# Pooled rows stored once a group, and the even and odd parts of a mixing stored apart and added by the loads

## The chip, the cores and the metric

The kernel runs on one core of a Trainium2 chip. A core has five engines that this text names as the profile does: PE (TensorE, matrix products; PEld are its weight loads), DVE (VectorE), ACT (ScalarE), POOL (GpSimd) and SP (SyncE, which here only issues transfers). Every engine works through its own queue in order, and semaphores hold an instruction until what it needs is there. Transfers run on 16 DMA engines; SP and POOL issue them. Matrix products land in PSUM, which has 8 banks; all else is in SBUF.

The metric is the device time of one execution in microseconds (us). The kernel before takes 1201.57 us (median of 3 runs, 1199.37 to 1205.03).

## The reference

Eight batches of 576 tokens, 8 heads of 64 channels. Each batch goes through attention of two kinds (over means of four neighbouring tokens, repeated four times; and local, within three tokens to either side), the real part of a two-dimensional Fourier transform added to the input, and a normalised feed-forward with 2048 hidden channels.

```python
q_d = q.reshape(B, H, Sd, factor, D).mean(axis=3)      # and k, v; factor = 4
out_d = sm_attn(q_d, k_d, v_d)
out_up = np.repeat(out_d, factor, axis=2)
scores = np.where(np.abs(pos[:, None] - pos[None, :]) < factor, scale * q @ k.T, -1e9)
x = (out_up + softmax(scores) @ v).transpose(0, 2, 1, 3).reshape(B, S, H * D)
X = np.fft.fft(np.fft.fft(x, axis=1), axis=2)
u = x + np.real(X)
un = (u - mean(u)) / np.sqrt(var(u) + 1e-06)
out = u + np.maximum(un @ w_ch1, 0.0) @ w_ch2
```

## The kernel before

**Two stages.** The first computes, batch after batch, the attention and the mixing (the Fourier part) and leaves three addends of u in DRAM: the pooled result `ud`, the local result `ux` and the mixed result `um`, each 577 rows of 512 channels. The second, the feed-forward, takes u in 9 blocks of 512 tokens, four tiles of 128 rows each. It loads a tile of `um` and lets two further transfers add `ux` and `ud` to it on the way in (`Block.load`, L715: part 0 is a plain load from SP, parts 1 and 2 are adding transfers that POOL issues with `accum_op`). Then it normalises and turns the tile (`stats`, `norm`, `turn`, L730 to L762) and runs 16 columns of hidden channels (`first`, `high`, `low`, `second`, L775 to L802). All matrix products of that stage have a high and a low part for precision.

**Pooled attention** (`Pooled`, L243): four steps of two heads; the result is gathered in the SBUF tile `odt` (two halves of 72 groups). `store` (L331) writes every group to four rows of `ud`, so that `ud` has a row for each token; `pack` (L341) moves part of `odt` for the mixing.

**Local attention** (`Unit`, L362): five units per batch, with results in `xa` (front half of the sequence) and `xb` (back half, mirrored).

**Mixing** (`Mix`, L514): sums and differences of the halves (L524, L527), folding of channels (`channels` L535, `fold` L548), a split into high and low (L559, L562), products along the sequence into `y` (L584), and products along the channels into PSUM banks `mix` (L616, L623). For each of three slots of rows there is an even and an odd bank. The token n and its mirror image are even plus odd and even minus odd: `even_out` (L627) copies the even bank to SBUF on ACT, and `unfold` (L631) makes sum and difference on DVE, reading the odd bank twice. Both read or write the two halves of a bank alternately, to bring the channels into their order. `store` (L643) writes them to `um`, front rows and mirrored rows, in ten transfers.

**Weights.** The feed-forward's weights come as 64 quarters of 64-bit words and are decoded on the way (`Quarter`, L138: ACT, POOL, three passes on DVE, ACT, POOL). Places for the first 3 of 16 columns exist from the start and are decoded during the first stage; the others follow when the first stage's memory is free (`close_a`, `close_e`, `close_d`).

**Order.** Every step is entered in a list with a number (`at(t, fn)`), and the list is sorted by it. The numbers come from the table `AT` at the head of the file. They are no times; they only set the order in which instructions stand in the engines' queues. `PACE` (20) is the distance of two batches in these numbers.

## Time and profile before

| | |
|---|---|
| median of 3 runs | 1201.57 us |
| profiled execution, whole | 1200.32 us |
| its span, first to last instruction | 1198.5 us |
| mean granted clock of PE | 0.972 |
| moved by DMA | 130.40 MB |
| 12 matrix products of one hidden column, L782, in the feed-forward | 2.72 us |

The profile gives for each engine its busy time, for each group of instructions the mean duration and what ended the idle time ahead of it, and for a stretch of time the busy time of all engines. A wait "PE tpn L753 <- DVE un L745" says that PE stood still until that DVE instruction was done. Tile names follow the program (`o` is the unfolded result, `ut` a tile of u, `un` the normalised tile, `tpn` its transpose, `hps`, `hh` and `hl` a hidden column with its high and low part). The rows themselves are shown in the prediction.

### The profile page before, as it was taken

Reading aid. Unit: us, or ns where it says so; the run is one execution under the profiler, and the core shown is the slowest. Engines: PE = TensorE matmul, PEld = TensorE weight load, DVE = VectorE, ACT = ScalarE, POOL = GpSimd, SP = SyncE. Lnnn points to the kernel's source line nnn. Section 1 sums busy time; section 2 is a strip of 40 time slices with the busy share of each in tenths; the row PEclk is TensorE's granted clock in tenths of the full one; section 3 lists DMA queues with packets and bytes.
Section 4 is the critical chain, followed back from the end, with each engine's and each line's share of the span. In section 5 each row is a group of like instructions: output and inputs, shape, how many; then the busy total and the mean of one; then the engine's idle time right before and its main releaser. Section 6 shows DMA issues by size and latency. Waiting matters only on the chain.

```text
span 1198.5 us, 20501 instructions
## 1 busy us (share of the span) xinstructions
PE 1128.4 (94%) x8224; PEld 949.5 (79%) x8224; DVE 590.6 (49%) x1234; ACT 363.7 (30%) x1054; POOL 307.7 (26%) x410
## 2 busy tenths in 40 slices
PE   4879988899976999999999999999999999999998
PEld 4768877888875788888888888888888888888887
DVE  3698999999878989632321321321321322222111
ACT  3556675667643444311111111111111111111010
POOL 2155436335547556320300200300200300200000
PEclk7889998999997999999999999999999999999999
DMA  8586777778868454160600600600600600600000
GB/s 270 176 249 200 223 227 232 196 226 277 204 159 200 103 161 125 60 141 1 141 1 1 141 1 1 141 1 1 141 1 1 141 1 1 141 1 1 36 1 36
DMA packets 61631, 130.40 MB, mean 109 GB/s; under 512 B 7560, under 2 KB 7688, under 8 KB 61280
## 3 DMA queue, kind: packets, MB, share of 16 engines
q1 hardware_dynamic: 48016, 99.30, 26.1%
q0 software_dynamic: 13520, 29.79, 14.3%
q8 instruction: 65, 1.06, 0.3%
q14 instruction: 30, 0.25, 0.1%
HBM read 90.13 MB, written 37.80 MB: 107 GB/s over the span
## 4 chain that ended last, share of the span: by engine, by line
PE 74%; DVE 11%; DMA 6%; issue 4%; POOL 2%; ACT 1%; SPq 1%; DVEq 0%; POOLq 0%; ACTq 0%
PE hps L782 32%; PE acc L802 11%; PE acc L800 11%; PE acc L801 11%; PE y L584 3%; DMA vsum<-in_vg_dram 2%; DVE w L535 1%; DVE o L636 1%; PE tpn L753 1%; DMA ux<-xa 1%; DVE xs L524 1%; PE av L462 1%; DVE sums L389 1%; DMA raw<-in_wq_dram 1%; PE sc L403 1%
## 5 line engine op out<-in xcount | busy, mean ns | idle before, releaser
L790 DVE SCALAR_TENSOR_TENSOR hl<-hps,hh 128x512 fp32r<-128x512 f32 x144 | 99.4, 691 | 463.0 <-ACT hh L786 463.0
L782 PE MATMUL hps<-unT,w1h 128*128 128x512 f32 x1152 | 311.6, 392 | 1.7 <-DVE unT L762 1.0
L782 PEld LDWEIGHTS hps<-unT,w1h 128*128 128x128 f32 x1152 | 215.1, 188 | 47.8 <-DVE unT L762 1.3
L786 ACT ACTIVATE hh<-hps 128x512 fp32r<-128x512 f32 x144 | 86.2, 598 | 543.4 <-PE hps L782 543.4
L800 PE MATMUL acc<-w2h,hh 128*128 128x512 f32 x576 | 226.4, 393 | 0.0
L802 PE MATMUL acc<-w2h,hl 128*128 128x512 f32 x576 | 225.1, 391 | 0.0
L801 PE MATMUL acc<-w2l,hh 128*128 128x512 f32 x576 | 225.0, 391 | 0.0
L782 PE MATMUL hps<-unT,w1l 128*128 128x512 f32 x576 | 155.2, 391 | 0.0
L782 PEld LDWEIGHTS hps<-unT,w1l 128*128 128x128 f32 x576 | 108.1, 188 | 23.8
L802 PEld LDWEIGHTS acc<-w2h,hl 128*128 128x128 f32 x576 | 108.2, 188 | 23.6
L800 PEld LDWEIGHTS acc<-w2h,hh 128*128 128x128 f32 x576 | 108.2, 188 | 22.8
L801 PEld LDWEIGHTS acc<-w2l,hh 128*128 128x128 f32 x576 | 108.2, 188 | 22.8
L738 POOL TENSOR_TENSOR rstd<-rstd,mhalf 128x1 f32<-128x1 f32 x36 | 20.4, 568 | 307.9 <-DVE rstd L737 306.9
L725 POOL DMA_DIRECT2D ut<-ux x40 | 35.7, 1106 | 205.7 <-DMA ut<-um 205.5
L421 ACT ACTIVATE sb<-sc,mx 128x64 f32<-128x64 f32 x320 | 70.0, 330 | 1.3
L403 PEld LDWEIGHTS sc<-qkT 64*64 64x64 f32 x1280 | 48.0, 146 | 3.8 <-issue 1.2
L462 PE MATMUL av<-vaug,pT 64*64 64x65 f32 x1280 | 46.7, 224 | 4.1 <-DMA vaug<-in_vw_dram 4.0
L762 DVE TENSOR_TENSOR unT<-tpn,unT 128x512 fp32r<-128x512 f32 x36 | 24.7, 687 | 51.3 <-ACT unT L759 51.3
L562 POOL TENSOR_TENSOR fl<-xeo,fh 128x512 fp32r<-128x512 f32 x32 | 44.8, 1401 | 13.7 <-ACT fh L559 13.7
L403 PE MATMUL sc<-qkT 64*64 64x64 f32 x1280 | 48.0, 230 | 0.0
L389 DVE TENSOR_REDUCE sums<-qkT 128x224 f32<-128x896 f32 (+4 forms) x48 | 43.2, 943 | 8.6 <-DMA qkT<-in_qk_dram 8.6
L462 PEld LDWEIGHTS av<-vaug,pT 64*64 64x64 f32 x1280 | 42.9, 140 | 5.4 <-DMA vaug<-in_vw_dram 4.5
(95 smaller groups left out, 1474.2 us busy)
## 6 DMA issues: line engine op xcount, KB each, us to landing
qkT<-in_qk_dram SPq DMA_DIRECT2D x40, 512.0 KB
raw<-in_wq_dram SPq DMA_DIRECT2D x64, 256.0 KB
vaug<-in_vw_dram SPq DMA_DIRECT2D x40, 260.0 KB
ud<-odt SPq DMA_DIRECT2D x16, 576.0 KB
out_dram<-ut SPq DMA_DIRECT2D x36, 256.0 KB
ut<-um SPq DMA_DIRECT2D x32, 256.0 KB
ut<-ux POOLq DMA_DIRECT2D x32, 256.0 KB, 5.7
ut<-ud POOLq DMA_DIRECT2D x32, 256.0 KB, 5.3
```

Source lines behind the costliest of these rows:

```text
L389: nc.vector.tensor_reduce(out=to, in_=x[:, :, a - g0 : e - g0], axis=AX.X, op=ALU.add)
L403: nc.tensor.matmul(sc[r, a * W : (a + 1) * W], self.qkT[r, 0, a // 2, o : o + W], self.qkT[r, 1, a // 2, o : o + W], start=False, stop=Tru ...
L421: nc.scalar.activation(out=self.sb[:, a], in_=self.sc[:, a * W : (a + 1) * W], func=AF.Exp, scale=0.125, bias=self.mx[:, a : a + 1],)
L462: nc.tensor.matmul(av[r, a, :], pT[r, 4 * hh + a], va[r, 4 * hh + a, :], start=True, stop=True)
L562: nc.gpsimd.tensor_sub(out=self.fl[:, t], in0=self.x[t], in1=self.fh[:, t].bitcast(F32))
L584: nc.tensor.matmul(y, l, r, start=(i == 0), stop=(i == len(mms) - 1))
L782: nc.tensor.matmul(hps, a[:, c, :], unT[:, x, c, :], start=(i == 0), stop=(i == len(mms) - 1))
L786: nc.scalar.activation(out=hh, in_=self.hps[f], func=AF.Relu)
L790: nc.vector.scalar_tensor_tensor(out=hl, in0=self.hps[f], scalar=0.0, in1=self.hh[f].bitcast(F32), op0=ALU.max, op1=ALU.subtract)
L800: nc.tensor.matmul(acc, hh, w2h, start=start, stop=False)
L801: nc.tensor.matmul(acc, hh, w2l, start=False, stop=False)
L802: nc.tensor.matmul(acc, hl, w2h, start=False, stop=stop)
```

## The change

Three things are changed.

1. `Pooled.store` writes each group once, to a `ud` of 144 rows. The load of the feed-forward reads every such row four times (a step of 0 in the access pattern).
2. `even_out` and `unfold` are replaced by `out`, which ACT runs: it copies the even bank once and the odd bank twice, the second time times -1. The even part goes to an array of its own, `ue` (289 rows), and plus and minus odd go to `um`. The middle row of the sequence falls away from one side, so that all arrays but `ue` have 576 rows. The load of a tile has four parts now: `ue` plain, then `um`, `ux` and `ud` adding (`PARTS = 4`).
3. The table `AT` has new numbers throughout.

```diff
-    "mix": (25.73, 25.9, 24.42, 25.37, 25.13),
+    "mix": (25.86, 25.59, 25.55, 25.23, 25.56),
...
-    "add": (17.46, 2.29, 3.72),
+    "add": (10.11, 2.63, 2.76),
...
+PARTS = 4
...
-    ud = [dram.tile([S + 1, DM], F32, name=f"ud{b}") for b in range(B)]
-    ux, um = ([dram.tile([S + 1, DM], F32, name=f"{n}{b}") for b in range(B)] for n in ("ux", "um"))
+    ud = [dram.tile([G, DM], F32, name=f"ud{b}") for b in range(B)]
+    ux, um = ([dram.tile([S, DM], F32, name=f"{n}{b}") for b in range(B)] for n in ("ux", "um"))
+    ue = [dram.tile([S // 2 + 1, DM], F32, name=f"ue{b}") for b in range(B)]
...
-            for t in range(2):
-                r0 = t * (HS + 1)
-                nc.sync.dma_start(
-                    out=ud[self.b][r0 : r0 + HS, :].rearrange("(g r) c -> g r c", r=4),
-                    in_=odt[:GH, t, :DM].unsqueeze(1).to_broadcast([GH, 4, DM]),
-                )
-            nc.sync.dma_start(out=ud[self.b][HS : HS + 1, :], in_=odt[GH - 1 : GH, 1, :DM])
+            nc.sync.dma_start(out=ud[self.b].rearrange("(t g) c -> g t c", t=2), in_=odt[:GH, :, :DM])
...
-        def even_out(self, t):
-            even = self.even[t] = pf.tile([P, DM], F32, name="even", bufs=2)
-            nc.scalar.copy(out=even[: slots[t][1]], in_=self.ps[t, 0])
-
-        def unfold(self, t, minus):
+        def out(self, t, odd, minus):
+
+            i = 1 + minus if odd else 0
             if t == 0:
-                self.o[minus] = pf.tile([P, NSL, DM], F32, name=f"o{minus}", bufs=1)
+                self.o[i] = pf.tile([P, NSL, DM], F32, name=f"o{i}", bufs=1)
             n = slots[t][1]
-            even, ps = (x.rearrange("p (two n) -> p n two", two=2) for x in (self.even[t][:n], self.ps[t, 1]))
-            nc.vector.tensor_tensor(
-                out=self.o[minus][:n, t].rearrange("p (n two) -> p n two", two=2),
-                in0=even,
-                in1=ps,
-                op=ALU.subtract if minus else ALU.add,
+            nc.scalar.mul(
+                out=self.o[i][:n, t].rearrange("p (n two) -> p n two", two=2),
+                in_=self.ps[t, odd].rearrange("p (two n) -> p n two", two=2),
+                mul=-1.0 if minus else 1.0,
             )
...
-            at(u + step + store, self.store, um, self.o)
+            at(u + step + store, lambda: self.store(ue, [self.o[0]]))
+            at(u + step + store, lambda: self.store(um, [self.o[1], self.o[2]]))
...
-                src = (um, ux, ud)[part][b][k0 : k0 + m, :]
+                if part == 0:
+
+                    m = min(m, HS - k0) if k0 < HS else m
+                    j = k0 if k0 < HS else k0 - HS + 1
+                    src = ue[b][j : j + m, :]
+                elif part < 3:
+                    src = (um, ux)[part - 1][b][k0 : k0 + m, :]
+                else:
+                    src = ud[b][k0 // 4 : (k0 + m) // 4, :]
+                    src = bass.AP(tensor=src.tensor, offset=src.offset, ap=[src.ap[0], [0, 4], src.ap[1]])
...
-                    at(starts[n] + 6 + 0.5 * i + 2.5 * part, blocks[n + 1].load, i, part)
+                    at(starts[n] + 6 + 0.5 * i + 1.5 * part, blocks[n + 1].load, i, part)
```

The order that comes out of the list is shown at three places. The first is ACT's queue while the sixth batch is mixed; `sb` and `sd` are the exponentials of the local and the pooled attention, `pT` and `ptd` copies of their transposes, `fh` the high part of a folded slot. Before:

```order
L629 COPY even<-mix 128x512
L572 CAST z<-odt 128x2
L559 CAST fh<-xeo 128x512
L419 ACTIVATE mx<-mx 128x8
L421 ACTIVATE sb<-sc,mx 128x64 x8
L276 ACTIVATE mxd<-mxd 72x4
L281 ACTIVATE sd<-sp,mxd 72x144 x4
L629 COPY even<-mix 128x512
L453 COPY pT<-tpl 128x512
L302 COPY ptd<-tp 72x288 x2
```

With the change (line numbers are those of the changed file; `o_5184` is the even part, the other two are plus and minus odd):

```order
L630 ACTIVATE o_5184<-mix 128x512
L416 ACTIVATE mx<-mx 128x8
L418 ACTIVATE sb<-sc,mx 128x64 x8
L630 ACTIVATE o_5224<-mix 128x512
L630 ACTIVATE o_5228<-mix 128x512
L279 ACTIVATE mxd<-mxd 72x4
L284 ACTIVATE sd<-sp,mxd 72x144 x4
L556 CAST fh<-xeo 128x512
L630 ACTIVATE o_5184<-mix 128x512
L450 COPY pT<-tpl 128x512
L630 ACTIVATE o_5224<-mix 128x512
L305 COPY ptd<-tp 72x288 x2
```

Where one copy of the even bank stood between two groups of exponentials, two copies of the odd bank follow it, the first pair right between `sb` and `sd`.

The second place is DVE's queue at the end of the first stage: the last slots of the last batch are folded (`xs`, `w`, `xeo`), the first block of the feed-forward gets its statistics and its normalised tiles `un`, and the seventh batch is unfolded. Before:

```order
L548 TENSOR_TENSOR xeo<-w 128x256
L524 TENSOR_TENSOR xs<-xa,xb 128x512
L734 BN_STATS st_5975<-ut_106 128x6
L735 BN_AGGR mv<-st_5975 128x2
L737 TENSOR_SCALAR rstd<-mv 128x1
L636 TENSOR_TENSOR o_5831<-even,mix 64x512
L636 TENSOR_TENSOR o_5833<-even,mix 64x512
L745 TENSOR_SCALAR un<-ut_103,mv,rstd 128x512
L535 TENSOR_TENSOR w<-xs 128x255
L535 TENSOR_TENSOR w<-xm 128x255
```

With the change:

```order
L545 TENSOR_TENSOR xeo<-w 128x256
L532 TENSOR_TENSOR w<-xs 128x255
L532 TENSOR_TENSOR w<-xm 128x255
L738 BN_STATS st_5996<-ut_114 128x6
L739 BN_AGGR mv<-st_5996 128x2
L741 TENSOR_SCALAR rstd<-mv 128x1
L545 TENSOR_TENSOR xeo<-w 128x256
L749 TENSOR_SCALAR un<-ut_111,mv,rstd 128x512
L749 TENSOR_SCALAR un<-ut_112,mv,rstd 128x512
```

The unfolding is gone, and the first normalised tile comes after the last folding instead of ahead of it.

The third place is POOL's queue at the handover, where it issues the additions for the second block's tiles (`ut_5951` to `ut_5954` before, `ut_5958` to `ut_5961` now), between the clamps `wt` and the low parts `w1l`, `w2l` of the weight decoding. Before, from the first additions to the second:

```order
L725 DMA ut_5953<-ux_66 128x512
L725 DMA ut_5954<-ux_66 128x512
L164 TENSOR_SCALAR wt<-wt 128x256
L193 TENSOR_TENSOR w1l_5962<-wt,w1h_5961 128x256
L164 TENSOR_SCALAR wt<-wt 128x256
L193 TENSOR_TENSOR w1l_5962<-wt,w1h_5961 128x256
L164 TENSOR_SCALAR wt<-wt 128x256
L725 DMA ut_5951<-ud_57 64x512
L725 DMA ut_5951<-ud_58 64x512
```

With the change, from the second additions to the third:

```order
L729 DMA ut_5960<-ux_66 128x512
L729 DMA ut_5961<-ux_66 128x512
L196 TENSOR_TENSOR w2l_5971<-wt,w2h_5970 128x256
L167 TENSOR_SCALAR wt<-wt 128x256
L196 TENSOR_TENSOR w2l_5971<-wt,w2h_5970 128x256
L167 TENSOR_SCALAR wt<-wt 128x256
L729 DMA ut_5958<-ud_57 64x1x512
L729 DMA ut_5958<-ud_58 64x1x512
```

Ahead of this piece stands a further group of five, for `um`, so that the five of `ud` come two clamps and two low parts later in the queue than before, and after ten other additions instead of five.

More of the change, by code (lines that the diff above doesn't have):

```diff
@@ L22 @@
 AT = {
-    "pooled": (-1.26, -1.46, -2.33, -2.53, -2.33),
-    "mix": (25.73, 25.9, 24.42, 25.37, 25.13),
-    "local_steps": (0, 1.47, 4, 5, 5.98, 8.33, 9.86),
-    "pooled_steps": (0, 1.18, 2.76, 4.04, 5.01, 7.14, 8.75),
-    "qk": (-10, 1.23),
-    "sums": (-2.83, 0.45),
-    "sum_v": (-10.41, -6.5, -3.44, 1.78),
-    "load_v": (4.22,),
-    "store_pooled": (0.83,),
-    "pooled_splits": (0.67, 1.6, 0.62, 0.96, 0.89, 1.28, 3.06),
-    "halves": (0.2, 1.82, -1.06, 1.66),
-    "splits": (0.89, 2.15, 0.3, 0.93, 0.62, 1.76, 2.52),
-    "z": (1.66, 5.51, 6.35, 6.73, 7.91),
-    "sequence": (8.13, 2.44, 0.74, 1.7),
-    "mixed": (16.48, 1.37, 1.17, 1.26, 1.31, 5.81),
-    "store_local": (1.87,),
-    "ffn": (5.97, 1.6),
-    "decode": (37.71, 6.9, 4.1, 1.25, 4.33),
-    "decode_steps": (-1.3, -0.25, 0.38, 2.09, 2.74),
-    "first_norms": (1.77, 1.54, 6.94, 0.87),
-    "second_norms": (0.62, 1.28, 3, 1.2),
-    "add": (17.46, 2.29, 3.72),
+    "pooled": (-1.41, -2.13, -2.53, -2.08, -2.33),
+    "mix": (25.86, 25.59, 25.55, 25.23, 25.56),
+    "local_steps": (0, 1.5, 4, 5.22, 6.36, 8.75, 10.11),
+    "pooled_steps": (0, 1.18, 2.29, 3.46, 4.56, 7.1, 8.75),
+    "qk": (-9.94, 1.51),
+    "sums": (-3.53, 0.27),
+    "sum_v": (-12.81, -9.36, 0.57, 2.2),
+    "load_v": (3.18,),
+    "store_pooled": (1.87,),
+    "pooled_splits": (0.57, 4.65, 0.32, 1.05, 1.04, 3.42, 4.78),
+    "halves": (0.3, 1.87, -1.3, 1.18),
+    "splits": (0.71, 2.15, 0.3, 0.59, 1.81, 2.46, 2.75),
+    "z": (1.06, 5.11, 6.1, 7.81, 9.01),
+    "sequence": (8.04, 2.24, 1.36, 1.52),
+    "mixed": (16.48, 1.35, 1.34, 0.77, 1.23, 5.7),
+    "store_local": (2.79,),
+    "ffn": (5.97, 1.61),
+    "decode": (34.88, 6.9, 3.53, 1.24, 3.62),
+    "decode_steps": (-0.95, -0.64, 0.38, 2.31, 2.97),
+    "first_norms": (4.11, 1.21, 9, 0.37),
+    "second_norms": (2, 1.04, 2.54, 1.7),
+    "add": (10.11, 2.63, 2.76),
 }
@@ L688, in plan @@
                 at(u, self.mix, i, 0)
-                at(u + even, self.even_out, i)
+                at(u + even, self.out, i, 0, 0)
                 at(u + step, self.mix, i, 1)
-                at(u + step + plus, self.unfold, i, 0)
-                at(u + step + minus, self.unfold, i, 1)
-            at(u + step + store, self.store, um, self.o)
+                at(u + step + plus, self.out, i, 1, 0)
+                at(u + step + minus, self.out, i, 1, 1)
+            at(u + step + store, lambda: self.store(ue, [self.o[0]]))
+            at(u + step + store, lambda: self.store(um, [self.o[1], self.o[2]]))
             at(4 * (NPAIR * self.b + NPAIR - 1) + AT["local_steps"][-1] + AT["store_local"][0], self.store, ux, (xa, xb))
@@ L879 @@
     for i in range(TILES):
-        for part in range(3):
+        for part in range(PARTS):
             at(120 + AT["add"][0] * part + 4 * i, blocks[0].load, i, part)
@@ L895 @@
             for i in range(TILES):
-                for part in range(3):
-                    at(starts[n] + 6 + 0.5 * i + 2.5 * part, blocks[n + 1].load, i, part)
+                for part in range(PARTS):
+                    at(starts[n] + 6 + 0.5 * i + 1.5 * part, blocks[n + 1].load, i, part)
                 v = starts[n] + 12 + i * (t - starts[n] - 18) / TILES
@@ L1029, in _tokens @@
     t = np.arange(SEQ)
-    return rows[:, np.where(t <= SEQ // 2, t, SEQ + SEQ // 2 - t)]
+    return rows[:, np.where(t < SEQ // 2, t, SEQ + SEQ // 2 - 1 - t)]
 def kernel(**inputs):
```

5 lines of the change are left out of this document (3 added, 2 removed).

## The prediction

> **What bounds the kernel now.** I read the page's busy row and its 40 slices first, to see where the time is.
>
> ```profile
> span 1198.5 us, 20501 instructions
> PE 1128.4 (94%) x8224; PEld 949.5 (79%) x8224; DVE 590.6 (49%) x1234; ACT 363.7 (30%) x1054; POOL 307.7 (26%) x410
> PE   4879988899976999999999999999999999999998
> DVE  3698999999878989632321321321321322222111
> PEclk7889998999997999999999999999999999999999
> ```
>
> Each slice is 30 us. From slice 14 on PE is full and DVE has time to spare: that is the feed-forward. Ahead of it, DVE reads 9 almost everywhere, and so does PE. In slice 12 (about 360 to 390 us) PE falls to 6 while DVE is still high. The windows give both stretches in numbers: attention and mixing, the handover, its end, and the feed-forward.
>
> ```profile
> core 0: us, PE busy (x) PEld busy (x) DVE busy (x) ACT busy (x) POOL busy (x), PEclk, DMA share, GB/s
> 0.00:353.00 353.00, 304.88 (x4528) 271.85 (x4529) 293.52 (x686) 214.80 (x757) 147.67 (x189) 0.93 0.77 220
> 353.00:369.00 16.00, 0.83 (x6) 0.61 (x5) 15.76 (x26) 1.82 (x4) 11.57 (x12) 0.63 0.86 248
> 369.00:417.00 48.00, 45.04 (x235) 37.78 (x234) 41.57 (x85) 21.20 (x51) 29.78 (x45) 0.95 0.56 132
> 417.00:1198.00 781.00, 777.62 (x3461) 639.26 (x3459) 239.79 (x441) 125.89 (x242) 118.64 (x166) 1.00 0.23 54
> ```
>
> In the last 781 us PE idles 3.4 us. Nothing that spares DVE can shorten that, so the change lives in the first 417 us. There I cut windows from one batch's zero-column product (L600, one per batch) to the next, which gives one period per batch:
>
> ```profile
> 73.55:117.64 44.09, 39.83 (x581) 35.31 (x581) 39.50 (x91) 29.48 (x107) 18.77 (x24) 0.96 0.72 214
> 117.64:158.80 41.16, 36.09 (x535) 32.13 (x532) 38.47 (x93) 26.43 (x91) 19.40 (x23) 1.00 0.80 238
> 158.80:202.92 44.12, 39.56 (x581) 35.02 (x582) 40.27 (x95) 28.45 (x100) 19.45 (x25) 0.93 0.76 217
> 202.92:246.25 43.33, 39.51 (x568) 35.01 (x566) 40.57 (x92) 26.80 (x94) 19.88 (x24) 0.91 0.75 214
> 246.25:285.43 39.18, 36.71 (x576) 33.27 (x575) 35.32 (x83) 26.82 (x96) 17.88 (x21) 1.00 0.80 228
> 285.43:325.89 40.46, 37.38 (x573) 33.51 (x574) 36.01 (x86) 26.32 (x94) 19.98 (x23) 1.00 0.87 243
> ```
>
> The first four periods also decode weights on DVE. They have 38.5 to 40.6 us of DVE in 41.2 to 44.1 us, 90 to 94%, and PE is nearly as full. The last two have 35 to 36 us of DVE and last 39 to 40.5 us. So the period follows DVE's load until PE's own work, 36.7 to 37.4 us at a full clock, stands in the way. ACT has 26 to 29 us and is free for a third of the time. The chain of waits, cut to 240 to 345 us, agrees: it runs through both engines in turn.
>
> ```profile
> by line: PE y L584 10.7%; DVE w L535 8.6%; DVE o L636 7.6%; issue 6.0%; DVE xs L524 5.2%; DMA ud<-odt 5.0%; DVE sums L389 4.9%; DMA odt<-odt 4.7%; DVE mxd L270 4.2%; PE av L462 3.7%; DVE xeo L548 3.3%; PE sp L265 3.0%; PE avd L310 3.0%; DVE
> ```
>
> The unfolding (DVE o L636) has 7.6% of these 105 us, 8.0 us in some 2.6 periods: about 3 us a period stand on the chain.
>
> Then comes the handover. In its 16 us DVE is busy for 15.76 and PE waits for one instruction of it:
>
> ```profile
> 368.52 0.87 PE L753 MATMUL tpn<-ident,un 128*128 128x128 f32 x3 [15.17 <-DVE un L745]
> 356.91 1.29 DVE L636 TENSOR_TENSOR o<-even,mix 128x512 f32<-128x512 f32 x2
> 365.55 1.29 DVE L636 TENSOR_TENSOR o<-even,mix 64x512 f32<-64x512 f32 x2
> 366.76 1.61 DVE L745 TENSOR_SCALAR un<-ut,mv,rstd 128x512 f32<-128x512 f32 x1
> ```
>
> **What the change costs and saves, part by part.**
>
> *The unfolding leaves DVE.* These are the passes that go, the pass that ACT makes now, and a DVE pass over PSUM in plain order:
>
> ```profile
> L636 DVE TENSOR_TENSOR o<-even,mix x48: 673/687/712, 99.3 to 416.3; 128x512 f32<-128x512 f32 x32, 64x512 f32<-64x512 f32 x16
> L629 ACT COPY even<-mix x24: 569/588/637, 97.8 to 409.1; 128x512 f32<-128x512 f32 x16, 64x512 f32<-64x512 f32 x8
> L806 DVE TENSOR_TENSOR ut<-acc,ut 128x512 f32<-128x512 f32 x44 | 27.6, 682 | 2.1 <-PE acc L802 2.1
> ```
>
> Six passes a batch at 0.687 us are 4.1 us less of DVE in each period. ACT gets nine passes a batch where it had three: six more at 0.588 us, 3.5 us, which takes it from 27.4 us (mean of the six rows) to about 31 of 40. The new passes read PSUM alternately from two halves. No ACT row shows that, so I bound it: 0.588 us (L629, plain order) below and twice that above. I take 0.588, because DVE's alternating pass (0.687) costs what its plain one does (0.682). The Trainium skill (SBUF — State Buffer, "Door 1: The DMA port swizzle") speaks against this: PSUM has 8-byte lines, and accesses that leave a line pay for it. By that the pass would come near the upper bound, which is the third rival below; the two DVE rows do not bear it out.
>
> The four decoding periods drop from a mean of 39.7 us of DVE to 35.6, which is the load of the two clean ones (35.3 and 36.0). I let them last what those last, 39.8 on average: 172.7 - 4 x 39.8 = **13.5 us** saved. The clean two drop to 31.5 us of DVE, and PE at 37.0 stays. Some of their 2.8 us above PE is latency that no lighter DVE removes, so I take half: 2 x 1.4 = **2.8 us**. The sum of both, 16.3 us in six periods, is 2.7 us a period, close to the 3 us that the chain gives. The bounds of these two terms together are 4 us, if PE's order is the limit already, and 172.7 + 79.6 - 6 x 37.0 = 30 us, if every period falls to PE's work.
>
> *The end of the front.* Up to 353 us the seventh period is a clean one, about 1 us. Then the chain on DVE loses the seventh batch's three pairs, which stand among the statistics and the last halves: 3 x 1.24 = 3.7 us. All of DVE's work there is queued in a row, so PE's 15.17 us shrink to about 11.5. What is late next is the last folding and the first normalisation, again on DVE. Together **4.7 us**, bounds 2 and 8.
>
> *Stores.* The pooled result is written once instead of four times, the mixing gets five more small stores per batch.
>
> ```profile
> 346.18 1.70 SPq L335 DMA_DIRECT2D ud<-odt  x2
> 347.93 1.56 SPq L339 DMA_DIRECT2D ud<-odt  x1
> 355.33 2.26 SPq L654 DMA_DIRECT2D ux<-xb  x4
> 357.64 0.43 SPq L655 DMA_DIRECT2D ux<-xb  x1
> ud<-odt SPq DMA_DIRECT2D x16, 576.0 KB
> 63.12 7.39 DMA ux<-xa
> ```
>
> SP loses about 2.4 us of issuing per batch (two of three pooled stores) and gains 2.7 (four stores and the row ahead). In bytes, 1.15 MB of pooled rows become 0.29, and the mixing grows by 0.59: slightly less traffic. In the chain of waits a store of the local result (7.39 us) stands behind the pooled one in the second batch; it may land sooner. I take **0**, with 3 us of gain and 2 of loss as bounds.
>
> *A fourth link in the loads.* Each tile of the feed-forward's input is now loaded once and added to three times, not twice. These rows show what one link costs:
>
> ```profile
> L725 POOL DMA_DIRECT2D ut<-ux x40: 806/1006/2127, 297.1 to 1027.7; - x40
> DMA to landing us min/median/max: 3.2/5.3/9.9
> DVE st L734 <- DMA ut<-ud: 4.7, 5, 1.5
> DVE hl L790 <- ACT hh L786: 463.0, 126, 4.9
> ```
>
> That is 1 us of POOL's time per addition and 5.3 us until it lands. In the feed-forward the first statistics of a block already wait for the last addition (5 waits, 4.7 us in all), so they come about 5 us later. Behind them on DVE stands hl for the next column. DVE idles up to 4.9 us ahead of nearly every hl, and PE runs another column in between, so I take **0** there. If that cover failed, the price would be up to 5 us in each of seven blocks.
>
> The second block's loads at the handover are the tighter place:
>
> ```profile
> 374.95 4.42 POOL L725 DMA_DIRECT2D ut<-ux  x5
> 384.93 2.62 POOL L725 DMA_DIRECT2D ut<-ud  x3
> 392.26 0.69 DVE L734 BATCH_NORM_STATS2 st<-ut 128x6 f32<-128x512 f32 x1
> 399.74 0.61 PE L753 MATMUL tpn<-ident,un 128*128 128x128 f32 x4
> ```
>
> POOL issues the first additions at 375, the second at 385; the statistics come at 392 and PE turns the result at 400. A third group between them puts five more issues (4.4 us), and with the clamps and low parts between groups 5 to 10 us, ahead of the statistics. The gap from 392 to 400 covers most of it. Behind the waiting statistics DVE queues weight decoding and hl, for which PE waits. Against it, the last batch's six passes leave DVE here too, 4 us, but PE idles only 3 us of the 48. I take a net **loss of 3 us**, bounds a gain of 3 and a loss of 10. By the Trainium skill (DMA: Bandwidth & Descriptors, "Anatomy of one DMA — SWDGE (gpsimd) path": 2 us fixed plus the bytes) an addition of 256 KB would land after some 2.6 us, an estimate from that page, and the loss would be nearer 1 us; the trace's 5.3 us decides.
>
> *The order of the stages.* PE's order in a period and the start up to 73 us keep their sequence but for swaps of neighbours; **0**, within the bounds above.
>
> **Sum:** -13.5 - 2.8 - 4.7 + 0 + 3 = -18.0 us. The profiled execution took 1200.3 us (span 1198.5 and 1.8 around it), so it becomes 1182.3. The median of the runs is 1.25 us above it: **1183.6 us**.
>
> **Rivals.**
>
> *PE is the limit already.* PE has 36 to 40 us in every period and its order is fixed. Then only the handover gains, 4.7, and about 4 of the periods, less 3: 1196 us. For it: PE is over 90% busy. Against it: the decoding periods are longer just where DVE has more, and in three of the four the clock of 0.91 to 0.96 says that PE pauses.
>
> *Everything falls to PE's work.* 30 us from the periods, 4.7 from the end, loads hidden: 1167 us. Against it: latency remains in any order.
>
> *ACT becomes the bound (slower).* If an alternating pass costs over 1.3 us, ACT gets 9 x 1.3 - 3 x 0.59 = 10 us more per batch, 37 to 39 in all, and the exponentials queue behind the passes. From that point a period exceeds today's, because PE waits for ACT's exponentials and for the banks. At 1.5 us a pass ACT has 39.1 us; with the 4 us that a period now adds to DVE's load, that is 43.1 against today's mean of 42.1, 8 us longer in eight batches, and the loads' 3 us on top: 1201.6 + 11 = 1212 us. For it: nine passes stand among the exponentials of three units. Against it: the DVE rows above.
>
> *The sums are not what is hidden.* The passes go to ACT, but the loads at the handover cost their full 10 us and the periods give only half: 1201.6 - 8 - 4.7 + 10 = 1199 us, no change.
>
> **How the numbers follow.** My forecast (1174 to 1193) gets 0.58, PE as the limit 0.12, PE's work alone 0.15, ACT as the bound 0.06, the loads 0.09. The range leaves out the slower rival and the tail of the best: 1168 to 1201. A measurement tells about 0.5% from no change, 6 us. Faster by more: the forecast, the best case, and a third of PE as the limit, and a little of the loads, 0.78. Within it: 0.15. Slower by more: 0.07.
>
> **What the new profile would show.** No DVE group at 0.69 us from mix; 72 ACT passes near 0.59 us (over 1.0 would mean the third rival). Windows from yz to yz near 39.8 us in the decoding batches and 38.4 after, with PE over 36 in each. PE's one long wait before tpn near 11 us instead of 15.2. In the handover, waits of DVE's statistics for the loads of ud, and a few us of PE behind them. Feed-forward stretch unchanged at 781 us from the second block on. I would be wrong if the periods stay at 41 to 44 while DVE's busy time falls, or if the waits of PE name ACT.

## The result and the profile after

The changed kernel takes **1243.59 us** (median of 4 runs, 1242.69 to 1244.84); the kernel before, run beside it, 1201.44. The ratio is 1.036, 95% interval 1.034 to 1.038: 42 us slower, where 18 us less were predicted. The two profiled spans differ by as much, 1241.5 against 1198.5 us.

Here is the page of the changed kernel: the busy row, and PE in 40 slices of 31 us.

```profile
PE 1145.1 (92%) x8224; PEld 954.6 (77%) x8224; DVE 559.4 (45%) x1186; ACT 385.7 (31%) x1102; POOL 346.4 (28%) x450
...
PE   4988999897878999999899999899899899999998
```

DVE lost what it should: 590.6 us became 559.4, ACT gained 22. But PE's row, which read 9 from slice 14 to the last but one, now falls to 8 four times in that stretch.

The windows of both kernels at the same four marks say where the 43 us of the profiles are: the first product of the feed-forward (hps), and the ends of its first three rounds' results (finish). First the changed kernel, then the one before.

```profile
0.00:377.88 377.88, 316.88 (x4566) 276.58 (x4566) 287.15 (x680) 239.81 (x812) 171.79 (x213) 0.94 0.76 213
377.88:457.88 80.00, 74.80 (x355) 60.74 (x355) 63.60 (x129) 36.10 (x87) 49.36 (x75) 1.00 0.64 159
457.88:514.66 56.78, 56.05 (x248) 46.35 (x248) 43.24 (x82) 22.41 (x54) 29.14 (x44) 1.00 0.31 89
514.66:1241.50 726.84, 697.41 (x3059) 570.96 (x3057) 165.37 (x299) 87.38 (x150) 96.05 (x121) 0.98 0.26 54
```

```profile
0.00:376.69 376.69, 312.73 (x4566) 278.11 (x4566) 315.72 (x721) 220.92 (x771) 163.88 (x207) 0.91 0.76 219
376.69:451.01 74.32, 72.03 (x347) 59.80 (x348) 64.73 (x132) 31.52 (x78) 45.32 (x69) 1.00 0.55 143
451.01:508.73 57.72, 57.72 (x256) 47.81 (x255) 44.52 (x85) 23.40 (x56) 29.50 (x45) 1.00 0.32 92
508.73:1198.50 689.77, 685.89 (x3059) 563.78 (x3057) 165.68 (x299) 87.87 (x150) 68.97 (x90) 1.00 0.21 46
```

The columns are those of the prediction's windows. The front is 1.2 us longer, though DVE has 28.6 us less in it; the handover is 5.7 us longer; and the last row, with the same 3059 products, is **37.1 us** longer. PE idles 29.4 us there instead of 3.9, and its products themselves take 11.5 us more at a mean clock of 0.98.

The groups of waits in the feed-forward (from 420 us on; total, times, longest) name the reason:

```profile
DVE st L738 <- DMA ut<-ud: 37.8, 7, 6.5
PE tpn L757 <- DVE un L749: 25.5, 7, 4.7
```

Seven waits of DVE's statistics for the last addition, seven of PE for what comes of them. One of the seven in order of time, POOL, SP, DVE and then PE of the changed kernel (start, length, engine, line, operation, and the wait ahead of it):

```profile
772.92 3.23 SPq L731 DMA_DIRECT2D ut<-ue  x6
778.42 3.46 POOL L729 DMA_DIRECT2D ut<-um  x4 [34.44 <-DMA ut<-ue]
782.70 0.89 POOL L729 DMA_DIRECT2D ut<-ux  x1 [0.82 <-DMA ut<-um]
787.68 0.95 POOL L729 DMA_DIRECT2D ut<-ud  x1
...
786.08 0.69 DVE L794 SCALAR_TENSOR_TENSOR hl<-hps,hh 128x512 fp32r<-128x512 f32 x1 [4.88 <-ACT hh L790]
793.24 0.69 DVE L738 BATCH_NORM_STATS2 st<-ut 128x6 f32<-128x512 f32 x1 [6.46 <-DMA ut<-ud]
795.08 0.55 DVE L749 TENSOR_SCALAR un<-ut,mv,rstd 128x512 f32<-128x512 f32 x1 [0.74 <-POOL rstd L742]
...
795.68 1.11 PE L757 MATMUL tpn<-ident,un 128*128 128x128 f32 x4 [4.69 <-DVE un L749]
```

The four links start at 772.9, 778.4, 782.7 and 787.7, some 5 us apart, and the statistics start 20.3 us after the first. They stand in DVE's order where three links (15 us) would have been enough: DVE waits 6.46 us. PE's next work, 4 transposes of that very tile, stands close behind in PE's order and cannot start: 4.69 us. It is not hl that PE waits for.

### The profile page after: what moved, and what is told of

It is laid out like the page before. It is cut to its first block, busy times and chain, and to the rows that moved or that the text cites. A ratio compares the mean times of both kernels' runs of the same rounds, so it can differ in the third digit from the quotient of the medians.

```text
span 1241.5 us, 20635 instructions
## 1 busy us (share of the span) xinstructions
PE 1145.1 (92%) x8224; PEld 954.6 (77%) x8224; DVE 559.4 (45%) x1186; ACT 385.7 (31%) x1102; POOL 346.4 (28%) x450
## 3 DMA queue, kind: packets, MB, share of 16 engines
q0 software_dynamic: 18768, 39.23, 18.3%
## 4 chain that ended last, share of the span: by engine, by line
PE 59%; DMA 15%; DVE 13%; POOL 5%; issue 4%; SPq 2%; ACT 2%; POOLq 0%; DVEq 0%; ACTq 0%
PE hps L786 23%; PE acc L804 8%; PE acc L805 8%; PE acc L806 8%; DMA ut<-ud 4%; DMA vsum<-in_vg_dram 3%; POOL ut L729 3%; DMA ut<-ue 2%; PE av L459 2%; PE y L581 2%; DMA ut<-ux 2%; PE sc L400 2%; DMA odt<-odt 1%; SPq L648 1%; PE tpn L757 1%
## 5 line engine op out<-in xcount | busy, mean ns | idle before, releaser
L804 PE MATMUL acc<-w2h,hh 128*128 128x512 f32 x576 | 230.9, 401 | 0.7 <-DVE ut L810 0.7
L806 PE MATMUL acc<-w2h,hl 128*128 128x512 f32 x576 | 228.1, 396 | 1.0 <-DVE hl L794 1.0
L805 PE MATMUL acc<-w2l,hh 128*128 128x512 f32 x576 | 228.6, 397 | 0.0
L729 POOL DMA_DIRECT2D ut<-um x40 | 37.8, 1101 | 210.0 <-DMA ut<-ue 209.2
L763 ACT CAST unT<-tpn 128x512 fp32r<-128x512 f32 x36 | 20.9, 584 | 127.9 <-PE tpn L757 127.9
L459 PEld LDWEIGHTS av<-vaug,pT 64*64 64x64 f32 x1280 | 42.2, 139 | 13.3 <-issue 11.6
L757 PE MATMUL tpn<-ident,un 128*128 128x128 f32 x144 | 24.6, 301 | 28.3 <-DVE un L749 26.9
L559 POOL TENSOR_TENSOR fl<-xeo,fh 128x512 fp32r<-128x512 f32 x32 | 47.3, 1478 | 5.3 <-ACT fh L556 5.3
```

What stands on the lines that cost most here:

```text
L459: nc.tensor.matmul(av[r, a, :], pT[r, 4 * hh + a], va[r, 4 * hh + a, :], start=True, stop=True)
L559: nc.gpsimd.tensor_sub(out=self.fl[:, t], in0=self.x[t], in1=self.fh[:, t].bitcast(F32))
L729: nc.gpsimd.dma_start(out=u[r0 : r0 + m], in_=src, accum_op=ALU.add)
L757: nc.tensor.transpose(tp[:, c * P : (c + 1) * P], self.un[i][:, c * P : (c + 1) * P], ident)
L804: nc.tensor.matmul(acc, hh, w2h, start=start, stop=False)
L805: nc.tensor.matmul(acc, hh, w2l, start=False, stop=False)
```

## The experiments

Each ratio is to the kernel before, run beside it on the same chip. Differences between two kernels are those of their ratios times 1200 us.

### The feed-forward: one link, one place

**e1_late_stats**, the changed kernel:

```diff
-                v = starts[n] + 12 + i * (t - starts[n] - 18) / TILES
+                v = starts[n] + 16 + i * (t - starts[n] - 22) / TILES
```

> The changed kernel with one edit: each block's statistics, normalisation and turn of the next block's first tile stand 4 units (6.8 us by 5.44 us per column of 3.2 units) later in the feed-forward. Theory A (the fourth link lands after the place of the statistics; DVE waits 4.2 to 6.5 us for ud, PE then 3 to 4.7 us at tpn): DVE's waits for ud fall from 41.8 to under 5 us, PE's waits for un vanish, blocks are 89.6 us apart again, and the time falls by the 37 us that seven blocks had grown: 1207 us (1203 to 1213). Rival B (the added loads slow PE's clock or the queues whatever the place): blocks stay at 93 to 96 us and the time within 8 us of 1244. Rival C (the wait only moves to the new place, because POOL issues the links late): half of the loss stays, near 1225.

Measured 1202.83 us, ratio 1.0006 (0.9977 to 1.0035): 42.7 us less than the changed kernel. That is more than the 37 us by which the feed-forward had grown; the two profiles differ in the front too (372.2 us to the first hps against 377.9), which the edit does not touch. One block, from finish to finish (its neighbours are alike):

```profile
659.20:748.83 89.63, 89.63 (x402) 73.73 (x401) 21.88 (x42) 11.71 (x20) 12.61 (x16) 1.00 0.28 59
```

PE is full again in 89.6 us; in the changed kernel such blocks take 92.9 to 96.0. All four links are still there, with the same bytes. Theory A holds; the queues and the clock (B) and a wait that moves along (C) do not.

**e2_before_link**, the kernel before with the fourth link alone:

```diff
-                for part in range(3):
-                    at(starts[n] + 6 + 0.5 * i + 2.5 * part, blocks[n + 1].load, i, part)
+                for part in range(4):
+                    at(starts[n] + 6 + 0.5 * i + 1.5 * part, blocks[n + 1].load, i, part)
...
-                src = (um, ux, ud)[part][b][k0 : k0 + m, :]
+                src = (um, ux, ud, ud)[part][b][k0 : k0 + m, :]
```

> The kernel before with one edit: from the third block on, each tile of the feed-forward's input gets a fourth load (the pooled rows are added a second time, so the input is not the reference's there), spaced 1.5 units as in the changed kernel. Nothing else of the change is in it. Theory A (the fourth link alone makes the loss): seven blocks grow from 89.6 to 93 to 96 us, time 1201 + 30 to 40 = 1231 to 1241. Rival (the loss needs the new order, the ACT passes or the smaller pooled rows): within 6 us of 1201.

Measured 1237.97 us, ratio 1.029 (1.027 to 1.031), 35 us more. Its waits from 420 us on:

```profile
DVE st L734 <- DMA ut<-ud: 38.1, 7, 5.7
PE tpn L753 <- DVE un L745: 25.8, 7, 4.0
```

These are the two groups of the changed kernel, in the kernel before, from one more load a tile. Nothing else of the change is needed for the loss.

**e3_before_early_stats**, the other way round, the place without the link:

```diff
-                v = starts[n] + 12 + i * (t - starts[n] - 18) / TILES
+                v = starts[n] + 9 + i * (t - starts[n] - 18) / TILES
```

> The kernel before with one edit: the same statistics and what follows them stand 3 units (5.1 us) earlier in each block of the feed-forward; three links as before. Theory A (only the distance between the landing of the last link and the place of the statistics counts): DVE waits some 5.5 us for ud and blocks grow by 3 to 6 us, time 1222 to 1240, though nothing of the change is in it. Rival (the number of links or DVE's idle time counts, not the place): within 6 us of 1201.

Measured 1201.61 us, 1.0002 (0.9979 to 1.0026). This says nothing against theory A, since the edit did more than it was meant to: at 9 units the first tile's statistics stand ahead of its last load (11 units) in the program, so they had only two links to wait for. **e9_early_stats_mended** puts all loads ahead:

```diff
-                    at(starts[n] + 6 + 0.5 * i + 2.5 * part, blocks[n + 1].load, i, part)
-                v = starts[n] + 12 + i * (t - starts[n] - 18) / TILES
+                    at(starts[n] + 6 + 0.5 * i + 1.5 * part, blocks[n + 1].load, i, part)
+                v = starts[n] + 9.1 + i * (t - starts[n] - 18) / TILES
```

> The kernel before once more with early statistics. In e3_before_early_stats the first tile's statistics stood ahead of its last load in the program, so they did not wait for it (and left out the pooled rows). Here the three loads of a tile are spaced 1.5 units as in the change, which puts all of them ahead of the statistics, and these stand 2.9 units (4.9 us) earlier. Theory A (only the distance between the last landing and the place of the statistics counts): DVE waits 4 to 6 us a block for ud, PE 2.5 to 4.5 at tpn, 1201 + 20 to 37 = 1221 to 1238. Rival (three links leave room enough, since the closer spacing lets them land earlier): within 6 us of 1201.

Measured 1235.11 us, 1.032 (1.026 to 1.038). DVE waits 35.1 us for ud from 420 us on, and PE 21.4 us at tpn. Three links and statistics 4.9 us earlier lose about what four links lose in the old place. What counts is the distance from the first load to the statistics, in links.

### The front: the order

**e4_old_order**: the code of the change, the table of the order from before (loads at the front 11.64 and 2.48 apart, so that four take the place of three).

```diff
-    "pooled": (-1.41, -2.13, -2.53, -2.08, -2.33),
+    "pooled": (-1.26, -1.46, -2.33, -2.53, -2.33),
...
-    "add": (10.11, 2.63, 2.76),
+    "add": (11.64, 2.29, 2.48),
```

> The changed kernel with the table of the order from before (the spacing of the early loads shrunk so that four take the place of three: 11.64 and 2.48). Theory A (the order is worth nothing in the feed-forward and costs some 10 us at the end of the front, through the local values that wait 8.6 us behind 15 mixing stores): blocks stay at 93 to 96 us, the end of the front gains: 1230 to 1240. Rival (the new table was needed for the new passes, and the old one delays PE by ACT's passes at other places): slower than 1244, 1250 to 1270.

Measured 1261.01 us, 1.047 (1.042 to 1.052): 13 us slower than the changed kernel. The rival was right: with the new passes and stores the old order is worse, and the new one earned these 13 us. A cut of the chain of waits of this run, from the first of a batch's fifteen mixing stores on SP to the last, and what follows:

```profile
168.06 0.41 SPq L648
...
179.16 6.57 DMA vaug<-in_vw_dram
185.86 2.00 PE av L459 x32
```

The local values stand on SP behind 11 us of stores, and PE behind the values. The changed kernel has that too, in its sixth period (SP's issues, then PE):

```profile
287.40 6.51 SPq L648 DMA_DIRECT2D ue<-o  x4
...
303.89 1.08 SPq L649 DMA_DIRECT2D um<-o  x1
305.02 3.42 SPq L372 DMA_DIRECT2D vaug<-in_vw_dram  x2
...
312.81 2.00 PE L459 MATMUL av<-vaug,pT 64*64 64x65 f32 x32 [8.57 <-DMA vaug<-in_vw_dram]
```

The fifteen stores hold SP from 287.4 to 305.0 us, and PE waits 8.57 us.

**e5_even_on_act** (on e1) and **e6_old_order_even_on_act** (on e4) take the five new stores off SP:

```diff
-            at(u + step + store, lambda: self.store(ue, [self.o[0]]))
+            at(u + step + store, lambda: self.store(ue, [self.o[0]], nc.scalar))
...
```

> The changed kernel with the later statistics of e1_late_stats, and the five stores of the even parts (ue) issued by ACT instead of SP, so that SP issues as many mixing stores a batch as before the change. Theory D (SP's issues stand in order, and the five added stores delay the local values and heads behind them): the periods shorten by up to 1 us each and PE's waits for vaug go; 1194 to 1200 against 1203. Rival P (PE's own work and small waits on DVE and POOL set the period in the new order; SP has room): within 3 us of 1203, or slower by the issues that ACT now makes (some 3 us a batch of an engine that has 30 of 41 us).

> The kernel of e4_old_order (the changed code in the order of before, 1261 us, first hps of PE at 395.3 us where before has 376.7) with the five stores of the even parts issued by ACT. Theory D (in the old order a burst of 15 mixing stores, 10.6 us of SP at 168 us, stands ahead of the local values and the heads, and is on the chain of waits with 20% of two periods): the first hps comes 12 to 18 us earlier and the time is 1243 to 1249. Rival (the ACT passes themselves are in the wrong place in the old order): the first hps stays within 5 us, time 1256 to 1266.

Measured 1215.86 us, 1.012 (1.008 to 1.015), and 1287.74 us, 1.072 (1.068 to 1.076): 13 and 30 us slower than their bases; e6 is slower than either forecast. Theory D was not tested by this, because ACT paid. A cut of ACT in e5:

```profile
171.80 3.47 ACTq L648 DMA_DIRECT2D ue<-o  x3
175.31 0.58 ACTq L649 DMA_DIRECT2D ue<-o  x1
175.93 0.42 ACT L587 CAST yh<-y 128x320 fp32r<-128x320 f32 x1 [5.55 <-DMA ue<-o]
```

ACT stands 5.55 us here until its own store lets it go on, and 42.2 us in seven such waits of 3.7 to 12.2 us in all. But it showed something else: ACT, busy for 31 of 41 us, does not hide such waits. So I asked for the price of each engine's time by itself.

### The front: what each engine's time is worth

**e7_dve_passes** and **e10_act_passes** (on e1) put six idle passes a batch on one engine:

```diff
+            if odd:
+                nc.vector.tensor_add(out=extra, in0=extra, in1=extra)
...
```

(e10: `nc.scalar.mul(out=extra, in_=extra, mul=1.0)`.)

> The changed kernel with the later statistics of e1_late_stats, and six idle additions of 128x512 a batch on DVE, one behind each odd pass of ACT, on a tile of their own that nothing reads: DVE has its old load again, 4 us a batch, and nothing waits for the passes but DVE's own queue. Theory of the prediction (the period follows DVE's load): 4 us a period, 1203 + 25 to 35 = 1228 to 1238. Rival P (PE and the order are the limit, DVE's spare time was not worth its length): 1203 + 0 to 8.

> As e7_dve_passes, but the six idle passes of 128x512 a batch go to ACT (scale by one, a tile of their own), one behind each odd pass: ACT has 3.5 us a batch more, 34 to 35 of 41 us. Theory T (the 3.5 us that the change itself put on ACT stand on the loop as those of DVE do, and took back what DVE gained): 1203 + 20 to 30. Rival of the prediction (ACT is free for a quarter of the period and hides them): 1203 + 0 to 6.

**e8_less_pe** and **e11_fewer_act** (on e1) take work away:

```diff
-                for i, (l, r) in enumerate(((lh, mh), (lh, ml), (ll, mh))):
+                for i, (l, r) in enumerate(((lh, mh), (lh, ml))):
...
```

```diff
-                at(u + step + minus, self.out, i, 1, 1)
             at(u + step + store, lambda: self.store(ue, [self.o[0]]))
-            at(u + step + store, lambda: self.store(um, [self.o[1], self.o[2]]))
+            at(u + step + store, lambda: self.store(um, [self.o[1], self.o[1]]))
```

> The changed kernel with the later statistics of e1_late_stats; of the mixing's three products per half the third (low part of y by the high matrix) is left out, 12 products a batch at 0.29 us, 3.5 us of PE. Theory P (PE's own work sets the period): 3 us a period, 1203 - 20 to 28 = 1175 to 1183. Theory S (the period is a loop through all engines, each of which waits in order; each engine's own work counts only where it stands on the loop): 1203 - 5 to 15.

> The changed kernel with the later statistics of e1_late_stats; the negated copy of the odd part is left out, and its stores write the plain copy, so ACT makes six passes a batch and not nine. Theory T: ACT loses 1.76 us a batch, 1203 - 8 to 14 = 1189 to 1195. Rival (ACT hides its passes): 1203 - 0 to 4.

**e14_half_unfold** and **e17_three_more** take three DVE passes a batch from the kernel before, and add three:

```diff
-                at(u + step + minus, self.unfold, i, 1)
-            at(u + step + store, self.store, um, self.o)
+            at(u + step + store, lambda: self.store(um, [self.o[0], self.o[0]]))
```

```diff
+            if minus:
+                nc.vector.tensor_add(out=extra, in0=extra, in1=extra)
```

> The kernel before without the difference of even and odd parts: three of the six unfolding passes a batch are left out, and both halves of the rows get the sum. VectorE has 2.06 us a batch less, 16.5 us in all; ACT, SP and the bytes are as before. Theory V (VectorE sets the front's length one for one): 1201 - 12 to 17. Theory of the prediction (part of it is latency that stays; 21 us for 33): 1201 - 8 to 11. Rival F (the order is fitted to the load it was made for, so added time costs and removed time gains little): 1201 - 0 to 5.

> The kernel before with three idle additions of 128x512 a batch on VectorE, one behind each difference of the unfolding, on a tile of their own: the mirror image of e14_half_unfold, which took three passes away for 4 us. Rival F (the order is fitted to its load: adding costs one for one, removing gains a quarter): 1201 + 13 to 20. Theory V2 (one price for both signs, that of e14): 1201 + 3 to 7.

| run | busy row of the engine, one profile each | time | ratio (interval) | against its base |
|---|---|---|---|---|
| e7, on e1 | DVE +37.0 us (560.8 to 597.8; 48 passes more) | 1234.84 | 1.028 (1.025 to 1.031) | +32 us |
| e17, on before | DVE +18.3 us (590.6 to 608.9; 24 passes more) | 1213.19 | 1.010 (1.006 to 1.013) | +12 us |
| e14, on before | DVE -8.9 us (590.6 to 581.7; 24 passes at 0.687 less, 16.5 us) | 1195.88 | 0.9963 (0.9942 to 0.9983) | -4 us |
| e10, on e1 | ACT +23.3 us (385.9 to 409.2; 48 passes at 0.637 more, 30.6 us) | 1213.2 | 1.012 (1.008 to 1.016) | +14 us |
| e11, on e1 | ACT -10.3 us (385.9 to 375.6; 24 passes at 0.6 less, 14 us) | 1196.43 | 0.9974 (0.9953 to 0.9996) | -4 us |
| e8, on e1 | PE -8.4 us (1137.5 to 1129.1; 96 products less) | 1199.83 | 1.001 (0.999 to 1.003) | 0 |

PE is not the limit, though it is the busiest engine of the changed front. But e8 took less from it than the 28 us that theory P counted, because products overlap. These rows of the kernel before show such a product and the one behind it, which starts 0.12 us later, not 0.28:

```profile
309.38 0.28 PE L623 MATMUL mix<-chanm,yl 128*128 128x256 f32 x1
309.50 0.40 PE L623 MATMUL mix<-chanm,yh 128*128 128x256 f32 x2
```

By that the 96 products are 11 us, an estimate from these rows, and PE's busy row fell by 8.4 us. None of it came back, by the two intervals 5 us at most. So theory P falls for the 8 to 11 us as well, and theory S, 5 to 15 us, was not met either.

DVE's time costs 0.6 to 0.9 of its length where it is added, in both kernels. Where passes are left out, half of what the busy row lost came back (4 of 8.9 us), or a quarter of the 16.5 us of the passes; by the interval it is 2 to 7 us. e17 is no exact mirror of that. Its idle passes mostly take as long as those of the unfolding, but some take up to 2.7 us, and DVE gained twice what it had lost in e14:

```profile
L645 DVE TENSOR_TENSOR extra<-extra x24: 668/680/2701, 103.4 to 438.6; 128x512 f32<-128x512 f32 x24
```

For one us of busy time, e17 gives a price of 0.4 to 0.9 by its interval and e14 one of 0.2 to 0.8. So it is not shown that removed time gains less than added time costs, nor that the order is fitted to its load, which would explain it. ACT's time costs 0.6 of its busy length (14 of 23.3 us). That a third of it comes back where it is taken away (4 of 10.3) isn't sure, since the intervals of e11 and e1 overlap. e10 and e17 fell between the ranges of their two theories.

### The front: the stores

**e12_fewer_stores** (on e1) stores the even parts in the first batch alone:

```diff
-            at(u + step + store, lambda: self.store(ue, [self.o[0]]))
+            if self.b == 0:
+                at(u + step + store, lambda: self.store(ue, [self.o[0]]))
...
-                    src = ue[b][j : j + m, :]
+                    src = ue[0][j : j + m, :]
```

**e16_even_on_pool** (on e1) issues them from POOL (the edit of e5 with `nc.gpsimd`). **e15_merged_stores** (on e1) makes one store of two where their slots agree:

```diff
-                    for lo, hi in ((4, 60), (60, 61)):
+                    for lo, hi in ((4, 61),) if first or to is ue else ((4, 60), (60, 61)):
```

> The changed kernel with the later statistics of e1_late_stats; the even parts are stored for the first batch alone, and all blocks load those, so SP issues five stores fewer in each of seven batches (some 3 us of its time a batch) and 4.1 MB less is written. Theory D (the added stores delay the local values and heads behind them on SP): 1203 - 8 to 20. Rival (SP has room in the new order): 1203 - 0 to 4.

> The changed kernel with the later statistics of e1_late_stats, and the five stores of the even parts issued by POOL (20 of 41 us busy, 0.9 us an issue) instead of SP; shapes and bytes unchanged. Theory D (SP's issues delay the local values and heads): 1203 - 3 to 8, as e12_fewer_stores less what POOL's own queue loses. Rival (the bytes cost): within 3 us of 1203. Third, as e5_even_on_act has shown for ACT: POOL waits in order for these issues, and its parts of the folding come late, 1203 + 5 to 15.

> The changed kernel with the later statistics of e1_late_stats; where the two stores of rows 4 to 60 and of row 60 cover the same slots (even parts, and the second halves of mixed and local parts) they are one store, six issues a batch fewer, with the same bytes. Theory D (the issues on SP cost): 1203 - 3 to 9. Rival (the bytes and the places cost, not the issues): within 2 us of 1203. Third: a store of 57 rows lands later than one of 56 and one of 1, and what waits for it is later: 1203 + 2 to 10.

Measured: e12 1192.6 us, 0.9935 (0.9908 to 0.9962), 8.5 us less than e1; e16 1199.78 us, 0.9976 (0.9943 to 1.0008), 3.6 us less than e1, though the two intervals overlap; e15 1312.6 us, 1.094 (1.090 to 1.098), 112 us more and far outside its three forecasts. So the five stores cost 8 us in all; taking them off SP alone brought less than half of it, and that half isn't sure. e15 was meant to test the issues and tested a shape; its chain of waits, and SP's waits for earlier stores of the even parts, show which:

```profile
166.24 12.57 DMA ux<-xb
...
179.19 17.41 DMA ue<-o
...
198.37 10.19 DMA vaug<-in_vw_dram
...
SPq L648 <- DMA ue<-o: 36.3, 9, 7.4
```

In the chain a later store on SP is released only 12.6 and 17.4 us after these 57-row stores. SP's stores wait 36.3 us in nine waits for earlier ones of the even parts, where e1 has 1.3 us, and PE waits 84.2 us in six waits for the local values.

**e13_pooled_once** is the pooled part of the change alone, in the kernel before: the new layout, one store a batch, the broadcast on the load; DVE unfolds as before, three links, the old order.

```diff
-            for t in range(2):
-                r0 = t * (HS + 1)
...
+            nc.sync.dma_start(out=ud[self.b].rearrange("(t g) c -> g t c", t=2), in_=odt[:GH, :, :DM])
...
+                if part < 2:
+                    src = (um, ux)[part][b][k0 : k0 + m, :]
+                else:
+                    src = ud[b][k0 // 4 : (k0 + m) // 4, :]
+                    src = bass.AP(tensor=src.tensor, offset=src.offset, ap=[src.ap[0], [0, 4], src.ap[1]])
```

> The kernel before, in its order, with the pooled part of the change alone: stored once a group, the rows shifted so that a group's four rows stand together, read four times by the load. The unfolding stays on VectorE, three links a tile, statistics where they were. Theory D (SP's issues are worth 0.3 of their time: e12_fewer_stores took 35 stores and 8 us): two stores a batch less, 16 in all, 1201 - 2 to 6. Rival (the broadcast read lands later than the plain one, and the feed-forward's statistics wait): 1201 + 5 to 35. The prediction had 0 here, within -3 to +2.

Measured 1196.55 us, 0.9969 (0.9948 to 0.9989). It is the one part of the change that was shown to pay, and the kernel to keep: 4 us faster than before, 47 faster than the changed kernel.

## Why the prediction was wrong, step by step

**The fourth link in the feed-forward, taken at 0: it cost 37 us (5.3 us a block), nearly all of the result.** This is the step that failed. The prediction saw that the first statistics already waited for the last addition, and that they would come 5 us later, and it gave the price if the cover failed: "up to 5 us in each of seven blocks". The cover it named was DVE's idle time ahead of hl, for which PE has another column to run. That cover is real. But it looked at one consumer only. The statistics' own result goes to PE too, as transposes (tpn) that stand less than two units behind in PE's order, and PE goes in order: 2.5 to 4.7 us of waiting a block. The row of the five waits (4.7 us) already said that the first statistics had no distance left; the question to ask was who else stands behind them. And "nothing that spares DVE can shorten that" was read as "nothing can happen there"; a full engine can still be made to wait.

**The decoding periods, -13.5 us: -4.2.** The windows from yz to yz after:

```profile
73.49:116.44 42.95, 37.87 (x572) 33.63 (x573) 35.32 (x87) 30.35 (x104) 20.67 (x24) 1.00 0.70 207
116.44:158.74 42.30, 38.58 (x573) 34.07 (x574) 36.43 (x90) 31.32 (x106) 19.86 (x25) 0.96 0.70 201
158.74:199.47 40.73, 37.79 (x577) 33.34 (x575) 35.80 (x86) 31.48 (x108) 21.11 (x25) 1.00 0.77 226
199.47:242.00 42.53, 38.48 (x577) 33.77 (x575) 36.61 (x85) 30.35 (x103) 20.03 (x26) 1.00 0.75 218
242.00:282.22 40.22, 38.99 (x574) 34.38 (x574) 35.34 (x85) 29.18 (x99) 18.12 (x20) 0.96 0.86 250
282.22:333.17 50.95, 41.35 (x578) 36.40 (x575) 31.59 (x80) 29.21 (x100) 21.78 (x26) 0.87 0.77 182
```

DVE has 36.0 us in the first four, as forecast (35.6), but they last 42.1 on average, not 39.8. The mechanism was right in one direction: DVE's time does set the period when it grows (e7). The mis-sized term is its price downward: four periods at a mean gain of 3.4 us each were expected from 4.1 us less of DVE, 0.8 for one; e14 measured 0.27 for one, counted in passes as there. And the other side was left out: six ACT passes more a batch were counted as free, and e10 and e11 (the latter not clear of the noise) price a us of passes at 0.27 to 0.45, 8 to 13 us for the 28 us that moved. The prediction had named its own sign of being wrong, periods that stay at 41 to 44 us while DVE's busy time falls; it came.

**The clean two, -2.8 us: +11.5.** One of them is the period of 50.95 us with PE's 8.57 us wait for the local values. In e1's profile, with the same front, this wait is 2.1 us in all and the two periods last 40.2 and 40.3 us, so its size varies from run to run.

**The stores, 0, bounds -3 to +2: outside on both sides.** The pooled store brought 4 us (e13), the five even stores cost 8 (e12). What was added up was SP's issuing time. Taking the five issues off SP (e16) brought back less than half of the 8 us, so the rest has another source, which stays open.

**The end of the front, -4.7 us: -6.1** (333.17 to 377.88, against 325.89 to 376.69). Right in size, though e1's profile has only -2.6 with the same front; but PE's long wait is now one for POOL's z, not 11 us for tpn. That row of PE, and one of DVE for the next point:

```profile
368.49 2.03 PE L597 MATMUL yz<-seqm,z 128*4 128x320 f32 x7 [9.04 <-POOL z L570]
...
399.02 0.69 DVE L738 BATCH_NORM_STATS2 st<-ut 128x6 f32<-128x512 f32 x1 [3.94 <-DMA ut<-ud]
```

**The loads at the handover, +3 us: +5.7**, inside the bounds, by the mechanism named: DVE's first statistics wait 3.94 us for ud. In e1's profile this stretch is 4.3 us longer than before.

**The order, 0:** wrong. With the new code the new order is worth 13 us (e4).

**The rivals.** "ACT becomes the bound" had the wrong price. The page has the 72 passes at 0.606 us, not 1.3; the plain pass before took 0.588, so the alternating read of PSUM cost next to nothing, and the two DVE rows decided rightly against the rule of the Trainium skill (SBUF — State Buffer, "Door 1: The DMA port swizzle"). But no threshold was needed: ACT's passes cost at 0.6 us too. "PE is the limit" does not hold by e8. "The loads at the handover" had the right object in the wrong place: the fourth link cost most where PE was full. An addition lands after 5.3 to 5.5 us, as before, so the 2.6 us worked out from the Trainium skill (DMA: Bandwidth & Descriptors, "Anatomy of one DMA — SWDGE (gpsimd) path") were too low.

What stays open: the separate prices (33 us of DVE at 0.27, -9; pooled store -4; ACT +8 to +13; even stores +8; handover +4) add up to 7 to 12 us, and e1 measures 1 us. In e1's profile the first hps comes 4.5 us earlier than before (372.2 against 376.7), where the three terms of the front had 21 us. The new order accounts for some of the rest; how much of it goes to which stage was not tried.

## What to carry to other kernels

In a stage in which one engine is full, a longer chain costs time as soon as it delays what that engine takes next: follow a delayed result to each of its consumers, the full engine first, and count in links from the first load to the place where the result is needed. Moving the place cost nothing here (e1 won back 43 us with one edit); so move the two together. And engine time has a price only on the loop it stands on: measure it with idle passes before you trade one engine's time for another's, and look in the busy row at what they came to: a pass on ACT cost time though ACT idled for a quarter of the period, and 96 products less on PE gained nothing.

## What the runs showed of the hardware

**After most waits of 2.5 to 4.7 us PE ran at a lower clock for some us, and the length of the wait does not say after which.** The seven waits of the changed kernel at tpn:

```profile
538.15 0.66 PE L757 MATMUL tpn<-ident,un 128*128 128x128 f32 x4 [3.00 <-DVE un L749]
605.77 1.11 PE L757 MATMUL tpn<-ident,un 128*128 128x128 f32 x4 [3.39 <-DVE un L749]
701.18 0.66 PE L757 MATMUL tpn<-ident,un 128*128 128x128 f32 x4 [3.05 <-DVE un L749]
891.27 1.12 PE L757 MATMUL tpn<-ident,un 128*128 128x128 f32 x4 [4.25 <-DVE un L749]
987.24 1.11 PE L757 MATMUL tpn<-ident,un 128*128 128x128 f32 x4 [4.68 <-DVE un L749]
1080.86 0.66 PE L757 MATMUL tpn<-ident,un 128*128 128x128 f32 x4 [2.47 <-DVE un L749]
```

With the one at 795.68 above, that is seven. The mean granted clock of the 8 us behind each is, in order of time, 0.79, 0.66, 1.00, 0.80, 0.80, 0.83 and 0.79; the kernel before, without such waits, has 1.00 from 500 to 1190 us. The stretches behind the waits of 3.05 and 2.47 us:

```profile
701.18:709.18 8.00, 8.00 (x38) 1.00 0.32 54
1080.86:1088.86 8.00, 8.00 (x30) 0.79 0.35 58
```

(Length, PE busy, granted clock, DMA share, GB/s.) The shorter wait was followed by the lower clock, the longer was not. In e2 the seven waits are 3.49 to 3.96 us long, and two of them were not followed by it. One of the two, with the 8 us behind it:

```profile
605.53 0.66 PE L753 MATMUL tpn<-ident,un 128*128 128x128 f32 x4 [3.51 <-DVE un L745]
605.53:613.53 8.00, 8.00 (x37) 1.00 0.28 43
```

The lower clock makes a wait dearer: in the changed kernel the block with the wait of 3.05 us grew by 3.2 us (92.86 against 89.64), that with 3.39 by 6.1 (95.75). The Trainium skill (TensorE: Matmul & The Clock Gate, "What's actually happening") puts the gate at an idle window of about 3.4 us that runs free of the kernel. These waits show no such limit on their own length: 3.51 us once were not enough, which a free window would allow, but 2.47 us once were, which it would not.

**Stores of 57 rows hold up the stores behind them, where pairs of 56 rows and one do not**: for 12.6 and 17.4 us in the chain of e15, for 228 to 342 KB a store, and SP's waits for the stores of the even parts are 36.3 us against 1.3 in e1. The Trainium skill (DMA: Bandwidth & Descriptors, "Why a DMA increments its semaphore by 16 and not by 1") says that a transfer is spread over the largest number of engines up to 16 that divides the slowest dimension of both its sides, which is the rows here: 14 for 56 rows, 3 for 57. The 112 us agree with that; how many engines took part, no view here shows.
